# Sliding-window attention with sinks, then a gated layer: other queues and another order for the first loads of v, w_in, w_out, q and k

## The chip, the cores and the metric

The kernel runs on one core of a Trainium2 chip. Time is device time in microseconds (us) for one launch; lower is better. Five engines work side by side, each through its own instructions in order: PE (matmuls), ACT (exp, tanh, copies), DVE (elementwise and copies), POOL (casts, masks, and DMAs that change the type on their way) and SP (plain DMAs). All DMAs share 16 DMA engines, whichever engine asked for them. They wait for each other by semaphores that the program sets.

## What is computed

Attention over q, k and v of shape (4, 8, 768, 64) in f32, where a query sees the first 4 keys (the sinks) and the last 128 keys up to itself, and then a layer of 2048 gated units over the 3072 rows of 512 values:

```python
keep = (pos[None, :] < 4) | ((rel >= 0) & (rel < 128))
scores = where(keep, q @ k.T / 8, -1e9)
a = softmax(scores)                      # row maximum taken off, sum + 1e-9
x = (a @ v).transpose(0, 2, 1, 3).reshape(3072, 512)
h = x @ w_in                             # (512, 2048)
out = (h * sigmoid(beta * h)) @ w_out    # (2048, 512)
```

## The kernel before

**Units and blocks.** The 3072 rows are 8 tiles of 384 rows (`TT`). Attention goes by units: unit `n` is two heads of one tile, four units to a tile, 32 in all. Units 0 to 3 are the first tile (first half of batch 0), units 4 to 7 the second. The layer goes by blocks: block `i` is one tile by 128 of the 2048 gated columns, 16 blocks to a tile, each four products of 128 by 128 by 384 with `w_in16` (`hidden_matmul`, one per chunk `c` of the 512 columns of x). `tanh` (ACT) and `gate` (DVE) follow, then `project` multiplies with `w_out16`.

**A unit's way.** q and k land in f32 (`load_qk`, on SP's queue), `cast` makes them bf16 (`qk16`, three buffers), `transpose_in` turns them on PE and copies them from PSUM to `qkT`; `scores` multiplies them and takes exp on ACT into `E`; units 0 to 3 get their mask added on PE (`add_mask`), units 4 to 7 multiplied in on DVE. `attend` multiplies `E` with `v_aug` (v and a column of ones, in bf16), `normalise` divides, and `transpose_out` turns the result into `xT`, chunk `c` of which comes from the tile's unit `c`. So a tile's first block needs all four units, the last of them for its product `c = 3`. Units of the second half of a batch also have a product with the sinks' keys (`scores_sink`, `k_sink`) and values (`v_sink`); from unit 12 on q and k come through other paths that the change leaves alone.

**The first loads.** SP asks for q and k of units 0 to 3 at once. POOL's queue, whose DMAs cast f32 to bf16 on their way, brings v of units 0 to 3 straight into `v_aug` (`load_v`, three DMAs), w_in in four DMAs of four blocks' columns each (`load_w_in`), the sinks (`load_sinks`), v of units 4 to 7 and w_out in eight DMAs of two blocks each (`load_w_out`). q and k of units 4 to 7 are asked for on SP when the first w_in DMA has landed. POOL also casts k of units 0 to 3 and q and k of units 4 to 11, and fills `k_sink` and the masks of units 4 and up. ACT casts q of units 0 to 3.

**The order.** `Prog.op` records each operation with what it reads and writes, an engine, and a guessed duration (`busy`, and `lag` until the result can be used). `Prog.round` then plays the program: always the operation that can start first, by the guesses, is put next in its engine's order, and `Prog.landings` plays the DMA queues (a fixed time from issue to first data, `QUEUE`; bytes at a guessed rate; a share between queues that are busy together). The played order becomes the program, so a changed guess can change the order on every engine. In the new order as in the old each engine then works strictly through its list. Where PE has nothing to do before the first block, matmuls on ones (`P.filler`) fill the gap that the plan expects; they are part of the program and run whether or not the gap is there.

The place where units 0 to 3 hand over to the blocks, before the change:

```python
    for i in range(2):
        with P.together("pe"):
            for c in range(3):
                hidden_matmul(i, c)
        P.fill_until = P.fill_until or P.nodes[-1]
    transpose_out(3, acc[0], "acc0", "act")
    sink_keys()
```

Of the kernel before, what the change touches and what calls it, by code (L numbers as in the profile page):

```python
# [18 lines left out]
TT = 384  # L19
# [5 lines left out]
HEAD1 = 32  # L25

# [47 lines left out]
class Node:  # L74
# [3 lines left out]
                 "place", "dma", "mode", "work", "hard")  # L78

    def __init__(self, id, eng):  # L80
        self.id, self.eng = id, eng
        self.items = []
        self.busy = self.lag = 0.0
        self.preds = {}
        self.succs = []
        self.open = 0
        self.ready = self.done = 0.0
        self.place = None
        self.dma = None
        self.mode = 128  # L90
        self.work = 0.0
        self.hard = set()


class Prog:
# [12 lines left out]
    QUEUE = {"sp": (1200.0, 1.0), "act": (1200.0, 1.0), "gp": (2100.0, 3.0)}  # L108
    TAIL, MIX, RING = 900.0, 1.07, 8
# [27 lines left out]
    def op(self, eng, fn, r=(), w=(), x=(), dma=None, busy=100.0, lag=None, after=(), mode=None,  # L137
           seq=None):
# [28 lines left out]
        if dma is not None:  # L167
            self.dma_count[dma] = self.dma_count.get(dma, 0) + 16
            node.dma = (dma, self.dma_count[dma])
            node.work = lag  # L170
# [22 lines left out]
    def landings(self, placed):  # L193
# [9 lines left out]
        while True:  # L203
            now, later = [], []
            for q, ns in queue.items():
                if head[q] < len(ns):
                    at = ns[head[q]].place + self.QUEUE[q][0]
# [6 lines left out]
            whole = sum(self.QUEUE[q][1] for _, q in now)  # L214
            rate = {q: (self.MIX if len(now) > 1 else 1.0) * self.QUEUE[q][1] / whole for _, q in now}
# [12 lines left out]
    def round(self, took, freed):  # L228
# [10 lines left out]
        def best(e):  # L239
# [9 lines left out]
            n = min(c, key=lambda n: (max(n.ready, free[e]), n.id))  # L249
            at = max(n.ready, free[e])  # L250
            if n.dma is not None and issued[e] >= self.RING and freed:
                at = max(at, freed[e][issued[e] - self.RING] if issued[e] - self.RING < len(freed[e]) else at)
            return at, n
# [100 lines left out]
def bass_streamingllm_window__then__act_swish_beta_kernel(  # L354
# [42 lines left out]
    stage = {t: [sb(f"{t}_stage{z}", (128, 2, 6, D), F32) for z in range(4)] for t in "qk"}  # L397
    land = [sb(f"land{z}", (128, 2, 2, 3, 2, D), BF16) for z in range(4)]
    qk16 = [sb(f"qk16_{z}", (128, 2, 3, 2, D), BF16) for z in range(NQK)]
    v_aug = sb("v_aug", (128, 4, 2, 6, D + 2), BF16)  # L400
    v_sink = sb("v_sink", (128, NPAIR, 2, D1), BF16)
    k_rows = sb("k_rows", (NPAIR, NSINK, 2, D), BF16)
    k_sink = sb("k_sink", (128, NPAIR, 128), BF16)
    qkT = [sb(f"qkT{z}", (128, 2, 2, TT), BF16) for z in range(4)]
    E = [sb(f"E{z}", (128, 2, 768), BF16) for z in range(2)]
    E_sink = [sb(f"E_sink{z}", (128, TT), BF16) for z in range(2)]
# [25 lines left out]
    def transfer(size, rate, busy=470.0):  # L432
        return {"busy": busy, "lag": size / rate}
# [8 lines left out]
    def constants():  # L442
        fill("dve", ones32[:, :], 1.0, ["ones32"])
        op("act", lambda e: e.activation(scratch[:, :], ones32[:, 0:1], AF.Exp, bias=0.0, scale=1.0),
           r=["ones32"], w=["scratch"], busy=1500.0)
        fill("dve", ones[:, :], 1.0, ["ones"])
        fill("dve", zeros[:, :], 0.0, ["zeros"], busy=350.0)
        P.filler = (lambda e: e.matmul(acc[1][:, 0:128], ones[:, :], ones[:, :], start=True, stop=True),
# [66 lines left out]
    def load_qk(n, x, after=(), queue="sp"):  # L515
# [5 lines left out]
           dma=f"{name}{pb}_{half}", seq="loads " + queue, **transfer(2 * TT * D * 4, 335))  # L521

    def load_v(T, c, after=()):
# [6 lines left out]
           dma=f"vb{kb}", **transfer(H * 128 * D * 4, 256, 900.0))  # L530

    def land_qk(n, x, after=()):

        b, hp, half, pb = place(n)
        for hh in range(2):
# [3 lines left out]
               dma=f"l{pb}{half}{x}{hh}", **transfer(TT * D * 4, 256, 780.0))  # L539

    def land_v(n, after=()):
        b, hp, _, pb = place(n)
        half = place(n)[2]
        for hh in range(2):
# [3 lines left out]
               w=[("v", pb, 3 * half + c, hh) for c in range(3)], after=after, dma=f"lv{pb}{half}{hh}", **transfer(TT * D * 4, 256, 780.0))  # L548
# [13 lines left out]
    def load_w_in(c, cs, m, ms, after=()):  # L562
        here = slice(m * 128, (m + ms) * 128)
        op("gp", lambda e: e.dma_start(w_in16[:, c:c + cs, here], w_in_src[:, c:c + cs, here]), after=after,
           w=[("w_in", cc, mm) for cc in range(c, c + cs) for mm in range(m, m + ms)],
           dma=f"wi{c}_{m}", **transfer(cs * ms * 128 * 128 * 4, 345, 740.0))

    def load_w_out(m, ms, after=()):
        op("gp", lambda e: e.dma_start(w_out16[:, m:m + ms, :], w_out_src[:, m:m + ms, :]), after=after,
           w=[("w_out", mm) for mm in range(m, m + ms)],  # L570
           dma=f"wo{m}", **transfer(ms * 128 * NOUT * 4, 345, 740.0))

    def load_sinks(after=()):
        s = k[:, :, 0:NSINK, :].rearrange("b (g h) s d -> (b g) h (s d)", h=2)
        for hh in range(2):
            op("gp", lambda e, hh=hh: e.dma_start(k_rows[:, :, hh, :].rearrange("n s d -> n s d"),
# [414 lines left out]
```

## Time and profile before

| what | value |
|---|---|
| three runs | 229.54, 230.21 (median), 231.41 us |
| the profiled execution | 229.27 us, of which the profile's span is 227.5 |
| PE busy | 219.9 us (97% of the span), 1759 matmuls |
| ACT, DVE, POOL busy | 141.9, 132.2, 128.6 us |
| moved by DMA | 28.53 MB; queue q0 (POOL's) 62352 packets, q1 (SP's) 34304, q10 (ACT's) 176 |
| the chain that ended last | PE 87%, DMA 7%, ACT 2% |
| PE granted clock | 1.00 throughout |

The profile is one execution. Its times count from the start of the span; a line of the timeline gives start, length, engine, source line, operation and tiles, and in brackets how long the engine stood idle before it and for what. A busy PE is not PE at its peak, since matmuls overlap: what they cost in a row is the distance from one start to the next (0.16 us for a product of a block, 0.216 for one with w_out).

Where the first stage stands, in the answers of the trace: the eight loads of SP are issued at 0.81 to 4.73 us and land between 3.5 and 10.8; the three v loads are issued at 2.91, 4.98 and 6.96 and land at 10.2, 11.5 and 12.4; the four w_in loads are issued between 8.26 and 12.10 and land at 14.9, 17.7, 21.0 and 24.9; q and k of units 4 to 7 are issued from 14.90 on and land between 21.5 and 29.7; the w_out loads are issued from 26.41 on and land between 33.1 and 43.5. The exps of units 0 to 3 run on ACT from 8.41 to 17.8, the first product with w_out starts at 33.54, and the first block of the second tile at 47.11.

### The profile page before, as it was taken

The numbers are of one execution on the slowest core, as the hardware profiler recorded it, in microseconds if no ns is written. First come the engines' busy times: TensorE is split into PE (matmuls) and PEld (weight loads), VectorE is DVE, ScalarE is ACT, GpSimd is POOL, SyncE is SP. The second block draws the span as 40 slices with busy tenths as digits, with TensorE's granted clock in tenths as the row PEclk, the third lists the DMA queues.
The fourth block names the chain that finished last, engine by engine and source line by source line (L and its number), as shares of the span: only waits on it lengthen the run. The fifth ranks groups of instructions, "written<-read, shape, count | busy, mean of one in ns | idle before, by whom it ended". The sixth has DMA issues, their size and how long they took to land.

```text
span 227.5 us, 4449 instructions
## 1 busy us (share of the span) xinstructions
PE 219.9 (97%) x1759; PEld 121.7 (53%) x1759; DVE 132.2 (58%) x261; ACT 141.9 (62%) x223; POOL 128.6 (57%) x190
## 2 busy tenths in 40 slices
PE   7798989999999999999999999999999999999995
PEld 5355555545555555555555555555555555555544
DVE  5455887569977666566555555665656555443300
ACT  3655886477787666657767666656675764545411
POOL 7788996799975969494939679594600000000000
PEclk9999999999999999999999999999999999999999
DMA  6999999999997999999999989899932202111022
GB/s 163 204 193 220 246 192 208 244 208 176 122 98 117 104 131 151 119 125 128 140 102 142 115 122 162 118 101 147 140 41 63 64 19 63 49 46 46 9 86 92
DMA packets 96853, 28.53 MB, mean 125 GB/s; under 512 B 83376, under 2 KB 93888, under 8 KB 96832
## 3 DMA queue, kind: packets, MB, share of 16 engines
q0 software_dynamic: 62352, 11.32, 65.5%
q1 hardware_dynamic: 34304, 16.79, 33.8%
q8 instruction: 14, 0.23, 0.4%
q10 hardware_dynamic: 176, 0.14, 0.2%
q14 instruction: 7, 0.06, 0.1%
HBM read 27.34 MB, written 6.29 MB: 148 GB/s over the span
## 4 chain that ended last, share of the span: by engine, by line
PE 87%; DMA 7%; ACT 2%; POOL 1%; SPq 1%; issue 1%; DVE 0%; ACTq 0%
PE acc L809 34%; PE h_ps L780 33%; DMA v_aug<-in_v_dram 6%; PE s_ps L736 5%; PE s_ps L693 4%; PE acc L780 2%; PE h_ps L809 2%; DMA k_stage<-in_k_dram 2%; PE s_ps L725 1%; PE s_ps L637 1%; PE s_ps L665 1%; SPq L520 1%; PE s_ps L619 1%; POOL land L538 1%; PE h_ps L665 1%; POOL qk L606 1%
## 5 line engine op out<-in xcount | busy, mean ns | idle before, releaser
L788 ACT ACTIVATE th<-h_ps,beta_half 128x384 f32<-128x384 f32 x120 | 69.5, 581 | 55.6 <-PE h_ps L780 55.1
L809 PE MATMUL acc<-w_out,g 128*128 128x512 bf16 x368 | 101.5, 380 | 0.0
L780 PE MATMUL h_ps<-xT,w_in 128*128 128x384 bf16 x480 | 96.8, 326 | 0.0
L801 DVE SCALAR_TENSOR_TENSOR g<-th,h_ps 128x384 bf16<-128x384 f32 x120 | 65.6, 549 | 45.7 <-ACT th L788 45.0
L780 PEld LDWEIGHTS h_ps<-xT,w_in 128*128 128x128 bf16 x480 | 46.4, 98 | 40.4 <-DVE g L801 0.5
L809 PEld LDWEIGHTS acc<-w_out,g 128*128 128x128 bf16 x368 | 32.8, 98 | 28.0 <-issue 4.0
L538 POOL DMA_DIRECT2D land<-in_q_dram x40 | 30.9, 773 | 28.5 <-DVE rden L745 28.5
L547 POOL DMA_DIRECT2D v_aug<-in_v_dram x40 | 30.9, 773 | 0.0
L538 POOL DMA_DIRECT2D land<-in_k_dram x40 | 30.9, 773 | 0.0
L701 ACT ACTIVATE E<-s_ps 128x1536 bf16<-128x1536 f32 x20 | 28.8, 1442 | 0.3 <-PE s_ps L693 0.3
L707 DVE TENSOR_TENSOR E<-E,mask 128x1536 bf16<-128x1536 bf16 x20 | 19.2, 958 | 16.1 <-ACT E L701 16.1
L817 ACT ACTIVATE out_sb<-acc 128x512 f32<-128x512 f32 x23 | 13.7, 598 | 10.2 <-PE acc L809 10.0
L736 PE MATMUL s_ps<-v_aug,E 128*128 128x65 bf16 x384 | 19.4, 193 | 0.6 <-DMA v_aug<-in_v_dram 0.6
L736 PEld LDWEIGHTS s_ps<-v_aug,E 128*128 128x128 bf16 x384 | 17.0, 97 | 4.7 <-issue 1.4
L747 DVE TENSOR_TENSOR o_norm<-s_ps,rden 128x384 bf16<-128x384 f32 x32 | 17.7, 555 | 0.9
L673 ACT ACTIVATE E<-s_ps 128x768 bf16<-128x768 f32 x16 | 13.0, 809 | 2.3 <-PE s_ps L665 1.9
L626 DVE COPY qkT<-s_ps 128x768 bf16<-128x768 bf16 x10 | 9.5, 955 | 5.8 <-PE s_ps L619 5.7
L693 PE MATMUL s_ps<-qkT 64*128 64x256 bf16 (+2 forms) x144 | 10.1, 254 | 0.0
L745 DVE RECIPROCAL rden<-s_ps 128x6 f32<-128x6 f32 x32 | 6.1, 192 | 6.6 <-PE s_ps L736 6.3
L680 DVE TENSOR_TENSOR E<-E,mask 128x768 bf16<-128x768 bf16 x16 | 9.1, 581 | 1.5 <-ACT E L673 1.4
L528 POOL DMA_DIRECT2D v_aug<-in_v_dram x9 | 8.2, 915 | 2.3 <-DMA w_in<-in_moe_w_in_dram 1.7
L619 PE MATMUL s_ps<-ident,qk 128*128 128x128 bf16 x72 | 7.4, 227 | 2.1 <-POOL qk L606 0.7
(65 smaller groups left out, 145.4 us busy)
## 6 DMA issues: line engine op xcount, KB each, us to landing
out_dram<-out_sb SPq DMA_DIRECT2D x23, 256.0 KB, 2.6
q_stage<-in_q_dram SPq DMA_DIRECT2D x12, 192.0 KB, 7.1
k_stage<-in_k_dram SPq DMA_DIRECT2D x12, 192.0 KB, 8.0
w_in<-in_moe_w_in_dram POOLq DMA_DIRECT2D x4, 512.0 KB, 8.6
w_out<-in_moe_w_out_dram POOLq DMA_DIRECT2D x8, 256.0 KB, 8.4
land<-in_q_dram POOLq DMA_DIRECT2D x40, 48.0 KB, 3.5
land<-in_k_dram POOLq DMA_DIRECT2D x40, 48.0 KB, 3.8
v_aug<-in_v_dram POOLq DMA_DIRECT2D x40, 48.0 KB, 3.4
```

The source lines that it names most:

```text
L538: op("gp", lambda e, d=d, s=s: e.dma_start(d, s), w=[("land", pb, half, x, hh)], after=after, dma=f"l{pb}{half}{x}{hh}", **transfer(TT * D ...
L547: op("gp", lambda e, d=d, s=s: e.dma_start(d, s), w=[("v", pb, 3 * half + c, hh) for c in range(3)], after=after, dma=f"lv{pb}{half}{hh}", ...
L693: op("pe", lambda e, at=at, w=w, kb=kb, qb=qb, nq=nq, hh=hh, rows=rows, bank=bank: e.matmul(s_ps[:, 2 * hh + bank, at:at + w], keys_of(pb, ...
L701: op("act", lambda e: e.activation(E[z][:, :, :], src, AF.Exp, bias=0.0, scale=SCALE), x=list(S_NAMES), w=[("E", z, 0), ("E", z, 1)], **ac ...
L707: op("dve", lambda e: e.tensor_tensor(E[z][:, :, :], E[z][:, :, :], m.unsqueeze(1).to_broadcast([128, 2, 768]), ALU.mult), r=[("E", z, 0), ...
L736: last=(x == len(kbs) - 1): e.matmul(av_ps[:, at + hh * D1:at + hh * D1 + D1], E[z][:, hh, col:col + 128], v_aug[:, pb, hh, kb, 0:D1], sta ...
L747: op("dve", lambda e: e.tensor_tensor(o_norm[o][:, :, :, :].rearrange("p m h d -> p (m h) d"), src[:, :, 0:D], rden[z][:, :].unsqueeze(2). ...
L780: op("pe", lambda e: e.matmul(bank, w_in16[:, c, m * 128:(m + 1) * 128], xT[:, c, T * TT:(T + 1) * TT], start=(c == 0), stop=(c == 3)), r= ...
L788: op("act", lambda e: e.activation(th[i % 3][:, :], bank, AF.Tanh, bias=0.0, scale=beta_half[:, m:m + 1]), x=[name], r=["beta"], w=[("th", ...
L801: op("dve", lambda e: e.scalar_tensor_tensor(g[T % 2][:, m, :], th[i % 3][:, :], 1.0, bank, ALU.add, ALU.mult), r=[("th", i % 3)], x=[name ...
L809: op("pe", lambda e: e.matmul(bank[:, 0:width], g[T % 2][:, m, t * 128:(t + 1) * 128], w_out16[:, m, cols], start=(m == 0), stop=(m == NM ...
L817: op("act", lambda e: e.activation(out_sb[z][:, 0:width], bank[:, 0:width], AF.Copy, bias=0.0, scale=0.5), x=[name], w=[("out_sb", z)], ** ...
```

## The change

v of units 0 to 3 is no longer cast by its DMA. Six DMAs on ACT's queue (`load_v32`: four heads by 128 rows each) bring it in f32 to a new tile `v_stage`, and four casts on POOL (`cast_v`, one a unit) put it into `v_aug`. The exp table's first use on ACT moves behind these issues. w_in comes in two DMAs of eight blocks each, asked for when unit 0's and unit 2's v have been cast; the sinks' keys are asked for after unit 1's. q and k of units 4 to 7, the sinks' values, the first w_out DMA and v of units 4 to 7 wait for unit 3's cast v; POOL's fill of `k_sink` and its masks too. The other w_out DMAs wait for the two w_in DMAs.

For units 0 to 3, the cast of q goes from ACT to DVE, and `transpose_first` takes the place of `transpose_in`: q and k are turned into two banks, q copied out by ACT and k by DVE. Scores use up to three pairs of banks, `attend` and `normalise` the bank `acc1`. The four `transpose_out` come together after the attention of unit 3, and the first three products of three blocks (before: two) follow them. The product with beta's transpose moves to the front. The sinks' tiles get a height of their own, `SINKS`, which is 128, as it was.

In `Prog`, the guesses for DMA rates and shares change (a weight for each DMA in place of one for each queue), and an operation that waits for room in a DMA ring is now compared by that time too. So the order of operations also moves where the text of the kernel does not, up to the first blocks of the second tile and a little beyond.

```diff
+SINKS = 128
...
-    QUEUE = {"sp": (1200.0, 1.0), "act": (1200.0, 1.0), "gp": (2100.0, 3.0)}
-    TAIL, MIX, RING = 900.0, 1.07, 8
+    QUEUE = {"sp": 1200.0, "act": 1200.0, "gp": 2100.0}
+    TAIL, MIX, HEAVY, RING = 900.0, 1.1, 2.5, 8
...
-            whole = sum(self.QUEUE[q][1] for _, q in now)
-            rate = {q: (self.MIX if len(now) > 1 else 1.0) * self.QUEUE[q][1] / whole for _, q in now}
+            weight = {q: queue[q][head[q]].weight for _, q in now}
+            mix = self.MIX if len(now) > 1 and max(weight.values()) > self.HEAVY else 1.0
+            rate = {q: mix * w / sum(weight.values()) for q, w in weight.items()}
...
+    def load_v32(x, c):
+        src = v[0, 4 * x:4 * x + 4, c * 128:c * 128 + 128, :].rearrange("h p d -> p h d")
+        op("act", lambda e: e.dma_start(v_stage[:, c, 4 * x:4 * x + 4, :], src), w=[("v_stage", x, c)],
+           dma=f"v{x}{c}", seq="loads act", **transfer(4 * 128 * D * 4, 240, 520.0, 0.45))
+
+    def cast_v(n):
+        op("gp", lambda e: e.tensor_copy(v_aug[:, n, :, 0:3, 0:D].rearrange("p h c d -> p c h d"),
+                                         v_stage[:, :, 2 * n:2 * n + 2, :]),
+           r=[("v_stage", n // 2, c) for c in range(3)],
+           w=[("v", n, kb, hh) for kb in range(3) for hh in range(2)], busy=460.0, lag=100.0)
...
-            eng = "act" if n < 4 and x == 0 else "gp"
+            eng = "dve" if n < 4 and x == 0 else "gp"
...
+    def transpose_first(n):
+        z = n % NQK
+        for which, name in enumerate("qk"):
+            bank, at = ((tr_ps, "tr"), (av_ps, "av"))[which]
...
+            eng = "act" if which == 0 else "dve"
...
-    load_v(0, 0, [ADD[0][0]])
...
-            load_v(0, n + 1, [("k16", n)])
-    load_w_in(0, 4, 0, 4, [("q_stage", 2, 0)])
...
+    for c in range(6):
+        load_v32(c // 3, c % 3)
...
+    cast_v(0)
+    load_w_in(0, 8, [("v", 0, 0, 0)])
+    cast(2)
+    cast_v(1)
+    load_sinks(1, [("v", 1, 0, 0)])
...
+    cast(3)
+    cast_v(2)
+    load_w_in(8, 8, [("v", 2, 0, 0)])
+    cast_v(3)
...
-                    load_qk(y, x, [("w_in", 0, 0)])
+                    load_qk(y, x, [("v", 3, 0, 0)])
+            fill("gp", k_sink[:, :, :], 0.0, ["k_sink"], busy=1800.0, after=[("v", 3, 0, 0)])
+            masks([("v", 3, 0, 0)])
+            load_sinks(0, [("v", 3, 0, 0)])
+            load_w_out(0, 2, [("v", 3, 0, 0)])
             for c in range(3):
-                load_v(1, c, [("w_in", 0, 4)])
+                load_v(1, c, [("v", 3, 0, 0)])
...
+    for n in range(4):
+        transpose_out(n, *((av_ps, "av") if n % 2 else (tr_ps, "tr")), "dve" if n < 2 else "act")
+    for i in range(3):
...
-            for m in range(0, 8, 2):
-                load_w_out(m, 2, [("q_stage", 0, 1)])
+            for m in range(2, 8, 2):
+                load_w_out(m, 2, [("w_in", 0, 0)])
```

In the order that comes out, PE does blocks 0 to 7, the transposes of the sinks' keys, the 12 transposes of units 4 and 5 and one sink score before block 8, the first that reads the second half of w_in; before, the transposes of unit 4 stood behind 14 blocks' worth of products (56). On POOL the order from unit 3's cast v is: fill of `k_sink`, masks, two sink DMAs, one w_out DMA, three v DMAs, then the casts of q and k of units 4 and 5, two w_out DMAs, and the casts of unit 6.

More of the change, by code (lines that the diff above doesn't have):

```diff
@@ L90, in __init__ @@
         self.mode = 128
-        self.work = 0.0
+        self.work, self.weight, self.late = 0.0, 1.0, 0.0
         self.hard = set()
@@ L248, in best @@
                 return None
[L249 to L253, printed above, removed]
+            out = issued[e] - self.RING
+            room = freed[e][out] if freed and 0 <= out < len(freed[e]) else 0.0
+            at = {n.id: max(n.ready, free[e], room if n.dma is not None else 0.0) for n in c}
+            n = min(c, key=lambda n: (at[n.id], n.id))
+            return at[n.id], n
         while any(n.place is None for n in self.nodes):
@@ L644, in keys_read, with scores @@
     def keys_read(pb, half, runs):
-        return [("qkT", pb, x) for x in sorted({half, *(kb // 3 for kb, _, _ in runs)})]
-    def scores(n, c, banks, names):
+        return [("qT", pb), *(("qkT", pb, x) for x in sorted({half, *(kb // 3 for kb, _, _ in runs)}))]
+    def scores(n, c, names):
+        src = h_ps if names[0] == "h0" else s_ps[:, 0:2, :] if names[0] == "s0" else s_ps[:, 2:4, :]
+        banks = [src[:, hh, :] for hh in range(2)]
         _, _, half, pb = place(n)
```

152 lines of the change are left out of this document (79 added, 73 removed).

## The prediction

> **What bounds the kernel now.** First the page's 40 slices, 5.69 us each: PE, DMA share and GB/s.
>
> ```profile
> PE   7798989999999999999999999999999999999995
> DMA  6999999999997999999999989899932202111022
> GB/s 163 204 193 220 246 192 208 244 208 176 122 98 117 104 131 151 119 125 128 140 102 142 115 122 162 118 101 147 140 41 63 64 19 63 49 46 46 9 86 92
> ```
>
> PE is full from the fourth slice to the last. The DMA engines are full in the first ten, so the start is a matter of transfers, and after it the end is set by PE's work. Next the chain of waits (start, length, what), at the place where attention of units 0 to 3 hands over to the products with w_in:
>
> ```profile
> 18.66 0.59 PE acc L780 x3
> 19.25 0.49 PE h_ps L780 x3
> 19.74 0.18 PE acc L764 x3
> 19.95 0.49 ACT xT L768
> 20.48 0.34 PE acc L780
> ```
>
> Six products (0.98 us) run early and the rest flows from 20.48: as if the stream had begun at 20.48 - 0.98 = 19.5. Then PE's timeline, for the transposes of q and k of units 4 and 5:
>
> ```profile
> 28.95 0.50 PE L619 MATMUL s_ps<-ident,qk 128*128 128x128 bf16 x6
> ...
> 30.66 0.51 PE L619 MATMUL s_ps<-ident,qk 128*128 128x128 bf16 x6
> ```
>
> and POOL's timeline, which casts their operands:
>
> ```profile
> 12.83 1.83 POOL L440 MEMSET k_sink<- 128x2048 bf16 x1
> ...
> 17.95 2.68 POOL L528 DMA_DIRECT2D v_aug<-in_v_dram  x3 [1.72 <-DMA w_in<-in_moe_w_in_dram]
> ...
> 24.11 0.50 POOL L606 CAST qk<-q_stage 128x384 bf16<-128x384 f32 x1
> ...
> 25.96 0.51 POOL L606 CAST qk<-k_stage 128x384 bf16<-128x384 f32 x1 [0.28 <-DMA k_stage<-in_k_dram]
> ```
>
> Unit 5's k lands at 25.9, is cast by 26.5 and is used at 30.66: 4 us of slack, because PE has 14 blocks (of 4 products) from four w_in chunks ahead of it. Last, the DMA queues (packets, MB, share) from 16.0 to 18.4 us
>
> ```profile
> q0 software_dynamic: 473, 0.47, 121.2%
> ```
>
> and from 19 to 22 us:
>
> ```profile
> q0 software_dynamic: 391, 0.39, 77.6%
> q1 hardware_dynamic: 397, 0.29, 39.7%
> ```
>
> SP asks for q of unit 4 at 14.90, yet its queue q1 moves nothing before 18.5: 3.6 us behind a busy q0 (3.6 again at 35.64). Then the two alternate one to one: 16 engines x 3 us / 394 = 122 ns for a pair of a 2 KB w_in row and a 768 B q/k row. A w_in row alone takes 16 x 2.4 / 473 = 81 ns. From 24 to 28 us q1 and the small v rows of q0 move 1158 and 1186 packets: 55 ns a pair.
>
> **The change, part by part.**
>
> *Start.* SP's eight loads are 2048 packets; v adds 3072 packets of 256 B on ACT's queue. No row has two hardware queues with such packets; alone a 768 B packet takes 34 ns (first load) and a 256 B one 20 (around 60 us), 54 together, and the pair above 55. At one to one and 55 ns, q and k end at 2.8 + 128 x 0.055 = 9.9 (before: 10.8) and the first three v loads at 2.8 + 96 x 0.055 = 8.1, landed 8.4. POOL then goes in order: cast v 0.50, w_in issue 0.75, cast v 0.50, k2 0.52, two k_rows issues 1.05, k3 0.52, cast v 0.50, w_in issue 0.75, cast v 0.50: 14.0. ACT issues seven DMAs of some 0.5 before its table load (1.28, 0.20), free at 5.9 instead of 2.8; its first copy is ready about then. The q casts (ACT, 0.51 each) go to DVE, with no row: 0.35 (L768) to 0.56 (L747), I take 0.4, beside other work. The 0.96 us qkT copy becomes two halves, ACT 0.48 and DVE 0.5. Unit 3's k cast ends at 12.2, and the rest follows from rows: transposes and copy 0.9, scores 0.4, two exps 1.5, attend 0.5, normalise 0.8, transposes and copy 0.7, and waits for the banks of units 1 and 2: unit 3's last transposes at 17.2, then six filler matmuls (0.34). First product at 17.6 against 19.5: 1.9 earlier (1 to 3).
>
> *w_in in two.* The first half (512 rows of 4 KB) is issued at 8.9 and moves from about 11.1 (2.2 us after the issue, as the first v load: 2.91, 5.1). The row's 404 GB/s (473 x 2 KB in 2.4 us) gives 5.2 us: landed at 16.9, just in time. The second half follows on the same queue.
>
> *What comes next is late.* The first half feeds eight blocks: 8 x 0.65 + 0.2 (sink keys) = 5.4, so PE gets to unit 4's transposes at 23.0. In the new order these, unit 5's and a sink score stand ahead of block 8. They need q and k of units 4 and 5, asked for at 14.0 (before 14.9), so moving from 17.6 on, now against 4 KB rows. No row shows such a pair: between 122 ns (if size did not matter) and 122 + 81 = 203; I take 203, as the row's time grows with its bytes. The second half has 512 / 16 = 32 rows per engine, of which 8 are gone by 17.6 (from 16.3 on, 0.162 each); 24 x 0.203 ends at 22.5, landed 22.9. q/k have then moved 24 of the 64 packets per engine they need. Beside w_out's first load (16 pairs x 0.122) they get 16 by 24.5, and beside v rows the last 24 x 0.055 by 25.8: unit 5's k lands at 26.1 (25.0, with 122 ns pairs, to 27.2, if q1 starts later by the doubled time of the rows ahead of it). POOL casts it by 26.6, PE is through at 27.1.
>
> The Trainium skill ("DMA: Bandwidth & Descriptors", section "Anatomy of one DMA — SWDGE (gpsimd) path") fits a POOL-issued DMA as 2.0 us plus its bytes at 436 GB/s. Over 2.1 MB that is 6.8 us, the first half landed at 15.7; with rows of 0.150 in the steps above unit 5's k would land 1.0 earlier and the time be 229.9, an estimate by that page. The 404 GB/s of this trace stand in the sum.
>
> POOL is no quicker way: from 14.0, memset 1.8, masks 2.9, v_sink 1.3, w_out 0.73, three v issues 2.65 put its first q cast at 23.4, the fourth cast at 25.4.
>
> *Sum.* At 27.1 PE has done 8 blocks, 12 transposes and a sink score (0.34 + 0.34 + 0.16 = 0.84). Before, at 28.95, it had 14 blocks. Six blocks are 3.9: the new kernel reaches the same work at 27.1 + 3.9 - 0.84 = 30.2, 1.2 behind. From 28.95 to 46.77 (unit 8's transposes) PE before has 24 transposes 1.35, 8 products 1.3, four sink scores 0.65, eight scores of 0.27, 32 products of 0.216, four attends of 0.57, 12 transposes 0.7: 15.35 in 17.82, so 2.5 lost. Afterwards I count 0.7 lost at unit 6's transposes (its casts stand behind two w_out issues, 1.45), 0.3 at unit 7's, 1.0 in the units' chain: 2.0 (1.0 to 3.0), 0.5 back. Later w_out chunks come about 1.3 us earlier, which no wait of before asks for: 0. Net +1.2 - 0.5 = +0.7 us: the 1.9 gained at the start runs into the wait at 23.0. SINKS is 128, as the tiles were: that part changes nothing.
>
> The profiled execution took 229.27 (span 227.5 and 1.8 around it); the sum is 230.0 against it. The median shown is 230.21, 0.94 above: on that scale **230.9**. Its own range takes -1.1 and +1.1 from the landing and -1.0 and +1.0 from the later losses, not all at once: 229.4 to 232.5.
>
> **Rivals.**
>
> *The loads are in time.* If q1 starts 1.2 us after its issue, as the very first load did (issued 0.81, moving at 2.0), and 4 KB rows go as pairs of 2 KB ones, then 64 pairs x 0.122 from 15.2 end at 23.0; POOL's casts decide, 25.4, PE is through at 25.7: 1.4 less, 229.5; with only 1.0 lost later 228.5, with nothing lost 227.5. For it: the 4 us slack before. Against: 3.6 us, twice.
>
> *PE falls back to half clock.* At the start 128-column matmuls stand 107 ns apart until 5.8, then 56 (the PEclk row shows nothing of it). From 23.0 to 27.1 PE has 0.84 us of work in 4.1. If that is idle enough, the next 4 us go at half speed: +2, 232.9, slower than before. Against: 7.95 to 9.75 held only six transposes, and they kept 56 ns. It decides once the wait passes about 3 us.
>
> The Trainium skill ("TensorE: Matmul & The Clock Gate", "Part 1: The HAM clock gate") puts the fall to half rate after one idle window of about 3.4 us. No row here has such a gap; by that rule the 2 us are due only if the wait is one piece of that length, and unit 4's transposes, from 23.9 on, would split it.
>
> *4 KB rows move worse.* At 330 instead of 404 GB/s a row takes 0.198: the first half is gone at 17.5, the second, paired, 31 x 0.239 later at 25.0, and the remaining q/k packets (16 x 0.122 and 17 x 0.055) at 27.9, 2.1 later than above: 233.0. For it: no row of this size. Against: 768 B and 2 KB rows alone run at 361 and 404 GB/s.
>
> **Chances and range.** Forecast 0.47, loads in time 0.27, half clock 0.14, worse rows 0.12. One per cent is 2.3 us, about what can be told here (three runs spread 1.9). Faster by over 1% (under 227.9): 0.12 of the second case and 0.03 of the first: 0.15. Slower (over 232.5): 0.06 of the first, 0.12 of the third, 0.12 of the fourth: 0.30. Within: 0.55. The range takes in most of the second case and most of the last two: 227.8 to 233.7, with some 0.1 left out on each side.
>
> **What would show it.** The first w_in product at 17.6 and the first half landed by 17; SP's fifth load asked at 14.0, nothing of q1 moving before 17.6; two q0 packets of 4 KB against two of q1 from then; PE waiting for POOL's casts from 23.0, block 8 about 27; 56 ns spacing held. A first product later than 19.5, or block 8 before 25, makes the forecast wrong.

## The result and the profile after

The changed kernel takes 232.03 us (median; 230.88 to 236.49), the kernel before 229.63 on the same chips (228.54 to 231.41): a ratio of 1.0101, 95% interval 1.0078 to 1.0124, so 1% slower. Two of its fourteen executions, 234.46 and 236.49, count as slow and are left out of the ratio. The profiled execution took 232.1 us (span 230.4), 2.8 more than the profiled one of before. The page's slices, 5.76 us each:

```profile
PE   7899699979999999999999999999999999999995
DMA  6999999999997999999998989999972112111022
```

PE has a thin fifth slice (23 to 29 us) where before it was full. The chain of waits shows what ends last in it (start, length, what; gaps left out):

```profile
20.75 0.49 PE acc L814 x3
21.23 0.97 PE h_ps L814 x6
...
22.41 1.17 ACT th L822 x3
...
26.50 0.59 ACT th L822
...
27.12 0.55 DVE g L835
27.67 0.88 DVE qkT L641
...
28.59 0.52 PE s_ps L634 x6
```

The first w_in products come at 20.6. The chain then leaves PE: it goes through ACT's tanh of blocks 0 to 7 and the last of DVE's gates for them, then DVE's copy of unit 4's transposes, and only then back to PE, which transposes unit 5. PE's timeline (start, length, what, and in brackets the idle time before it and what ended it):

```profile
20.58 0.65 PE L814 MATMUL acc<-xT,w_in 128*128 128x384 bf16 x3
...
26.24 0.50 PE L634 MATMUL s_ps<-ident,qk 128*128 128x128 bf16 x6
28.59 0.51 PE L634 MATMUL s_ps<-ident,qk 128*128 128x128 bf16 x6 [1.85 <-DVE qkT L641]
28.94 0.33 PE L670 MATMUL s_ps<-qkT,k_sink 128*128 128x384 bf16 x1
29.10 0.81 PE L814 MATMUL acc<-xT,w_in 128*128 128x384 bf16 x4
```

Units 4 and 5 are transposed into the same bank of PSUM (tr), the memory that PE writes its results to. Unit 5's transposes must wait until DVE has copied unit 4's out of it; DVE runs in order and has the gates first; and block 8, whose weights landed at 24.94, stands behind unit 5 on PE. Before, two blocks lay between the two units (28.95 and 30.66) and hid the same copy, as PE's and DVE's timelines of the kernel before show:

```profile
29.29 0.81 PE L780 MATMUL h_ps<-xT,w_in 128*128 128x384 bf16 x4
29.94 0.81 PE L780 MATMUL acc<-xT,w_in 128*128 128x384 bf16 x4
29.65 0.95 DVE L626 COPY qkT<-s_ps 128x768 bf16<-128x768 bf16 x1
```

POOL's timeline of the changed kernel shows how near the casts were:

```profile
27.21 0.51 POOL L621 CAST qk<-k_stage 128x384 bf16<-128x384 f32 x1 [0.53 <-DMA k_stage<-in_k_dram]
```

Unit 5's k is cast by 27.7, 0.9 before PE can use it. The same kernel profiled a second time (232.31 us, span 230.6) took another way to the same end:

```profile
18.48 0.65 PE L814 MATMUL acc<-xT,w_in 128*128 128x384 bf16 x3
...
24.57 0.34 PE L634 MATMUL s_ps<-ident,qk 128*128 128x128 bf16 x3 [0.27 <-POOL qk L621]
25.42 0.34 PE L634 MATMUL s_ps<-ident,qk 128*128 128x128 bf16 x3 [0.51 <-POOL qk L621]
26.81 0.94 PE L634 MATMUL s_ps<-ident,qk 128*128 128x128 bf16 x6 [1.05 <-DVE qkT L641]
27.55 0.53 PE L670 MATMUL s_ps<-qkT,k_sink 128*128 128x384 bf16 x1
27.87 1.49 PE L814 MATMUL acc<-xT,w_in 128*128 128x384 bf16 x4
```

Here the start is 2.1 earlier, PE waits for casts and for the copy, and then four products take 1.49 instead of 0.81: half rate. The windows view has a granted clock of 0.50 from 26.82 to 30.23 and 1.00 on both sides. The page's clock row (tenths of full rate per slice) shows it in the fifth and sixth slice:

```profile
PEclk9999889999999999999999999999999999999999
```

PE also begins at half rate in every profile used here: 128-column matmuls stand 107 ns apart and later 56. The change came at 13.0 us in profile 1 and between 6.1 and 7.4 in profile 2; the page's clock row does not show this one.

To compare all runs, I worked out from PE's records when the same amount of matmul work was reached (columns streamed, fillers left out; 27 to 28 records that are missing in each trace but before's are counted by the program's order), as time behind the kernel before (profile 1 is the execution of 232.10 us, profile 2 that of 232.31):

```
reached before at us    24.6   26.7   28.9   44.2   46.8    end
changed, profile 1     +1.5   +3.5   +3.3   +2.2   +3.3   +2.9
changed, profile 2     -0.6   +3.4   +3.2   +2.2   +3.5   +3.1
qk_early               +0.7   +2.7   +2.4   +1.4   +2.8   +2.4
fill_wait              -0.4   +1.7   +2.0   +1.1   +1.7   +1.8
filler_more            -0.7   +3.9   +5.0   +4.0   +5.3   +4.9
w_in_four              -0.6   -0.2   -0.5   -1.2   -0.9   -0.7
order_only             +0.8   +0.9   +0.6    0.0   -0.6   -0.7
order_qk2              -0.8   +0.2    0.0   -0.8   -1.3   -1.4
```

One stretch makes most of the loss, from 24.6 to 26.7 on that scale: +2.0 in one profile, where a late start had made 1.5 before it, and +4.0 in the other. What follows gives back some of it and takes some again.

### The profile page after: what moved, and what is told of

It is laid out like the page before. It is cut to its first block, busy times and chain, and to the rows that moved or that the text cites. A ratio compares the mean times of both kernels' runs of the same rounds, so it can differ in the third digit from the quotient of the medians.

```text
span 230.4 us, 4457 instructions
## 1 busy us (share of the span) xinstructions
PE 219.8 (95%) x1748; PEld 123.7 (54%) x1775; DVE 132.2 (57%) x264; ACT 141.3 (61%) x224; POOL 125.5 (54%) x189
## 4 chain that ended last, share of the span: by engine, by line
PE 86%; ACT 5%; DVE 3%; issue 3%; DMA 2%; POOL 0%; SPq 0%; ACTq 0%; POOLq 0%
PE acc L843 33%; PE h_ps L814 32%; PE s_ps L770 5%; PE s_ps L727 4%; ACT th L822 3%; PE s_ps L700 2%; DMA k_stage<-in_k_dram 2%; PE h_ps L843 2%; PE s_ps L759 1%; PE acc L450 1%; PE s_ps L670 1%; PE s_ps L798 1%; DVE g L835 1%; PE s_ps L634 1%; DVE E L714 1%
## 5 line engine op out<-in xcount | busy, mean ns | idle before, releaser
L843 PE MATMUL acc<-w_out,g 128*128 128x512 bf16 x341 | 94.8, 380 | 1.7 <-issue 0.6
L561 POOL DMA_DIRECT2D v_aug<-in_v_dram x40 | 30.9, 774 | 0.0
L735 ACT ACTIVATE E<-s_ps 128x1536 bf16<-128x1536 f32 x20 | 28.9, 1443 | 0.0
L770 PE MATMUL s_ps<-v_aug,E 128*128 128x65 bf16 x336 | 16.8, 193 | 0.8 <-DVE E L714 0.7
L770 PEld LDWEIGHTS s_ps<-v_aug,E 128*128 128x128 bf16 x336 | 15.1, 97 | 4.2 <-issue 1.3
L781 DVE TENSOR_TENSOR o_norm<-s_ps,rden 128x384 bf16<-128x384 f32 x28 | 15.5, 555 | 0.8
L714 DVE TENSOR_TENSOR E<-E,mask 128x768 bf16<-128x768 bf16 x16 | 9.8, 615 | 1.0 <-ACT E L707 0.7
L621 POOL CAST qk<-k_stage 128x384 bf16<-128x384 f32 x12 | 6.1, 511 | 5.9 <-DMA k_stage<-in_k_dram 5.9
L759 PE MATMUL s_ps<-v_sink,E_sink 128*128 128x130 bf16 x48 | 9.3, 219 | 0.0
L779 DVE RECIPROCAL rden<-s_ps 128x6 f32<-128x6 f32 x28 | 5.4, 192 | 6.0 <-PE s_ps L770 6.0
L727 PEld LDWEIGHTS s_ps<-qkT 64*128 64x128 bf16 x144 | 4.9, 94 | 7.1 <-issue 6.4
```

What stands on the lines that cost most here:

```text
L561: op("gp", lambda e, d=d, s=s: e.dma_start(d, s), w=[("v", pb, 3 * half + c, hh) for c in range(3)], after=after, dma=f"lv{pb}{half}{hh}", ...
L727: op("pe", lambda e, at=at, w=w, kb=kb, qb=qb, nq=nq, hh=hh, rows=rows, bank=bank: e.matmul(s_ps[:, 2 * hh + bank, at:at + w], keys_of(pb, ...
L735: op("act", lambda e: e.activation(E[z][:, :, :], src, AF.Exp, bias=0.0, scale=SCALE), x=list(S_NAMES), w=[("E", z, 0), ("E", z, 1)], **ac ...
L770: last=(x == len(kbs) - 1): e.matmul(av_ps[:, at + hh * D1:at + hh * D1 + D1], E[z][:, hh, col:col + 128], v_aug[:, pb, hh, kb, 0:D1], sta ...
L781: op("dve", lambda e: e.tensor_tensor(o_norm[o][:, :, :, :].rearrange("p m h d -> p (m h) d"), src[:, :, 0:D], rden[z][:, :].unsqueeze(2). ...
L843: op("pe", lambda e: e.matmul(bank[:, 0:width], g[T % 2][:, m, t * 128:(t + 1) * 128], w_out16[:, m, cols], start=(m == 0), stop=(m == NM ...
```

## Experiments

Line numbers in the experiments' profiles are shifted by a few where lines were added. Every ratio is to the kernel before on the same chip. The expectations name theories: by 'start' v's new way slows the first loads, and late operands of unit 5 hold block 8; by 'DVE order', which came after qk_early, DVE's late copy holds it.

**filler_more**: more fillers before 14 us, at the same places.

```
-                    for _ in range(int((start - at - 60.0) * 0.8 / cost)):
+                    count = int((start - at - 60.0) * 0.8 / cost)
+                    for x in range(count):
                         f = Node(-1, "pe")
-                        f.items.append((fn, None, [self.filler[2]]))
+                        more = (count + 1) // 2 if x == count - 1 and at < 14000.0 else 0
+                        f.items.extend([(fn, None, [self.filler[2]])] * (1 + more))
```

> The changed kernel with each run of filler matmuls before 14 us half as long again (written out at the same places, the order of everything else as it is), so that PE has fewer gaps. Rival 'half clock': PE goes to 56 ns a 128-column matmul at 6 to 9 us instead of 13, the first product moves from 20.6 to 19.6 or earlier, and the time falls by 1 us or more, to 231 or less. Theory 'start': PE may be at full rate sooner, the first product may gain 0.3 to 0.8, but unit 4's and 5's casts stay at 24.7 to 27.2 and block 8 at 29.0 to 29.2; the time stays within 0.4 of the changed kernel's 232.0.

Measured: 232.51 us (1.0119, 1.0078 to 1.0160). The first product came at 18.38 (20.58 in profile 1), and the time did not fall, not even in the three executions whose granted clock stayed at 1.00 (231.81, 232.34 and 232.49): the start's half rate is not what the change costs. PE's timeline, of an execution of 234.12 us and so the slowest of its set, shows where the gain went:

```profile
26.05 0.34 PE L636 MATMUL s_ps<-ident,qk 128*128 128x128 bf16 x3 [1.54 <-POOL qk L623]
27.45 0.83 PE L636 MATMUL s_ps<-ident,qk 128*128 128x128 bf16 x6 [1.05 <-DVE qkT L643]
28.07 0.53 PE L672 MATMUL s_ps<-qkT,k_sink 128*128 128x384 bf16 x1
28.39 1.49 PE L816 MATMUL acc<-xT,w_in 128*128 128x384 bf16 x4
```

The wait for casts and copy grew by what the start gained, and half rate followed it, longer than in the changed kernel.

**qk_early**: SP's loads of q and k of units 4 to 7 wait for unit 0's cast v; the order on every engine is unchanged.

```
-                    load_qk(y, x, [("v", 3, 0, 0)])
+                    load_qk(y, x, [("v", 0, 0, 0)])
```

The wait was exchanged after planning, so that the planner could not answer it.

> The changed kernel with one wait changed: SP's loads of q and k of units 4 to 7 wait for unit 0's cast v instead of unit 3's; the order on every engine is the same. They are asked for at about 9.6 us instead of 15.4. Theory 'start': the loads then move beside both w_in halves, some 0.2 us a pair of rows; unit 5's k lands by 20 instead of 27.2, the first w_in half 0.8 to 2 later (19.7 to 21 for 18.9), and block 8, freed of the wait, at 27.0 to 27.8 instead of 29.1; time 1.2 to 2.0 less than the changed kernel's: 230.0 to 230.8. Rival 'order': block 8 is earlier but the time is not, since later waits take it: within 0.5 of 232. Rival 'w_in': the first half now comes so late (after 22) that the first product is held by it and the time is as long or longer.

Measured: 231.68 us (1.0079, 1.0041 to 1.0117). Unit 5's k landed at 19.91, 7 us earlier, yet PE's timeline is the old one:

```profile
19.75 0.66 PE L818 MATMUL acc<-xT,w_in 128*128 128x384 bf16 x3 [1.29 <-DMA w_in<-in_moe_w_in_dram]
...
25.41 0.50 PE L638 MATMUL s_ps<-ident,qk 128*128 128x128 bf16 x6
27.77 0.51 PE L638 MATMUL s_ps<-ident,qk 128*128 128x128 bf16 x6 [1.85 <-DVE qkT L645]
28.11 0.33 PE L674 MATMUL s_ps<-qkT,k_sink 128*128 128x384 bf16 x1
28.27 0.81 PE L818 MATMUL acc<-xT,w_in 128*128 128x384 bf16 x4
```

The wait at unit 5 is the same 1.85 us, though POOL, which now waited for no load, had cast the last operand by 25.8 (23.89 to 25.8 for the four casts, as the prediction reckoned for POOL alone: 23.4 to 25.4). Block 8 is 8.52 behind the first product here and in profile 1 of the changed kernel (29.10 - 20.58). This ended my theory that late loads hold block 8. (The second w_in half landed at 26.73 here, still ahead of the 27.77 at which unit 5's transposes began.) DVE's timeline shows the copy straight behind the last gate:

```profile
24.99 1.20 DVE L839 SCALAR_TENSOR_TENSOR g<-th,h_ps 128x384 bf16<-128x384 f32 x2
26.29 0.55 DVE L839 SCALAR_TENSOR_TENSOR g<-th,acc 128x384 bf16<-128x384 f32 x1
26.76 0.95 DVE L645 COPY qkT<-s_ps 128x768 bf16<-128x768 bf16 x1
```

**w_in_four**: four w_in DMAs of four blocks, two at each place.

```
-    load_w_in(0, 8, [("v", 0, 0, 0)])
+    for m in (0, 4):
+        load_w_in(m, 4, [("v", 0, 0, 0)])
```

> The changed kernel with w_in in four DMAs of four blocks instead of two of eight, two issued at each of the two places; the planner then puts units 4's and 5's transposes behind blocks 9 and 11 instead of in front of block 8. Theory 'start': the first product stays near 20 (unit 3's chain, not w_in, holds it), but PE has blocks 8 to 11 to do while unit 4's and 5's q and k come, so most of the wait of 26 to 29 us goes: 1.0 to 1.8 less, 230.2 to 231.0. Rival 'w_in size': if 4 KB rows were what makes the loads late, 2 KB rows should land the first blocks' weights earlier and the first product moves to 19 or earlier. Rival 'no effect': the wait only moves behind block 11, within 0.5 of 232.

Measured: 229.31 us (0.9979, 0.9953 to 1.0006), 2.7 less than the changed kernel and more than expected. Two things differ: the DMAs, and the order that the planner makes of them. The next run parts them.

**order_only**: all DMAs as in the changed kernel; the planner alone is told a higher rate for the second w_in half. Its own schedule had that half landing at 27.1 (the traces: 24.4 and 24.9), and unit 5's k at 23.1 (the traces: 26.6 and 27.2), and so put units 4 and 5 ahead of block 8; with 23.9 it puts unit 4 behind block 8 and unit 5 behind block 11.

```
+        rate = 400 if m == 0 else 800
...
-           dma=f"wi{m}", late=0.0 if m else 800.0, **transfer(DM * ms * 128 * 4, 400, 740.0, 3.0))
+           dma=f"wi{m}", late=0.0 if m else 800.0, **transfer(DM * ms * 128 * 4, rate, 740.0, 3.0))
```

> The changed kernel with every DMA as it is (w_in in two of 4 KB rows, the same waits); only the planner is told that the second w_in half comes sooner, so that it puts unit 4's transposes behind block 8 and unit 5's behind block 11 instead of both in front of block 8. Theory 'DVE order': the wait at unit 5's transposes goes (under 0.5 us), block 8 follows block 7 at once, 5.4 to 6 behind the first product, and the time falls by 1.7 to 2.7: 229.3 to 230.3, as the kernel with four w_in DMAs did (229.31). Rival 'w_in size': it is the four DMAs that made that kernel fast; here block 8 waits for the second half (landed 24.9) and the time stays above 231.2. Rival 'half clock': no stretch at half rate was in that profile, so no part of it.

Measured: 228.27 us (0.9961, 0.9940 to 0.9983), 3.8 less than the changed kernel's first set, 4.3 less than its second (232.56, beside this one on the same chip), 1 us more than was expected, and faster than the kernel before. PE's timeline:

```profile
19.93 0.65 PE L815 MATMUL acc<-xT,w_in 128*128 128x384 bf16 x3
...
24.94 1.46 PE L815 MATMUL acc<-xT,w_in 128*128 128x384 bf16 x8
26.24 0.50 PE L635 MATMUL s_ps<-ident,qk 128*128 128x128 bf16 x6
26.58 1.46 PE L815 MATMUL h_ps<-xT,w_in 128*128 128x384 bf16 x8
27.88 0.81 PE L815 MATMUL acc<-xT,w_in 128*128 128x384 bf16 x4
28.53 0.50 PE L635 MATMUL s_ps<-ident,qk 128*128 128x128 bf16 x6
```

No row has an idle time: block 8 begins at 25.59, 5.7 behind the first product, and three blocks lie between units 4 and 5 while DVE copies (26.94 to 27.9). The loads are those of the changed kernel (unit 5's k landed at 26.27, the second half at 24.04). So order alone takes the loss away, and two DMAs of 4 KB rows are no worse than four. By the table the profiled executions of the two orders lie 3.6 apart: 0.7 is there by 24.6 (the starts), 2.0 comes in the stretch to 28.9, and 0.9 behind it, where the order differs too. No run gave unit 5 a bank of its own, which would try the bank without the order.

**v_by_pool**: v of units 0 to 3 by POOL's three casting DMAs as before, w_in still in two.

```
-    for c in range(6):
-        load_v32(c // 3, c % 3)
+    load_v(0, 0, [ADD[0][0]])
...
-    cast_v(0)
-    load_w_in(0, 8, [("v", 0, 0, 0)])
+    load_w_in(0, 8, [("q_stage", 2, 0)])
...
-    cast_v(2)
-    load_w_in(8, 8, [("v", 2, 0, 0)])
-    cast_v(3)
+    load_w_in(8, 8, [("k16", 0)])
```

The other two load_v stand between the casts as before; SP's loads for units 4 to 7 wait for the first w_in half, POOL's fill, masks and later loads for unit 0's cast k.

> Undoes the v part: v of units 0 to 3 comes by POOL's three casting DMAs as before the change, with no v on ACT's queue and no cast v on POOL; the two w_in DMAs wait for unit 2's q and unit 0's k cast, q and k of units 4 to 7 for the first w_in half; the rest is the changed kernel. Theory 'start': v's 256 B rows on a second hardware queue slow the first loads, these delay POOL's casts, issues and SP's asks, and unit 5's late q and k then hold block 8. By it q and k of units 0 to 3 land by 10.9 us again (12.5 in the changed kernel), the first product with w_in is at 19.0 to 19.8 (20.6), and the time is 1.5 to 2.5 us less than the changed kernel's, 229.5 to 230.5. Rival 'half clock': PE's half speed until 13 us is the cost; it goes away here only if PE is busier at the start. Rival 'order': the planner's new order on PE and the new constants cost the time whatever the loads do: within 0.5 of 232.

Measured: 230.30 us (1.0038, 1.0009 to 1.0067), in the range that theory 'start' gave, with its first product at 18.20, earlier than that. But the planner also put unit 4's q transposes ahead of block 5, so this says little of v's route. Its profiled execution (232.41, well above the median) has PE waiting and then at half rate:

```profile
24.91 0.34 PE L634 MATMUL s_ps<-ident,qk 128*128 128x128 bf16 x3 [2.15 <-POOL qk L621]
25.09 2.29 PE L814 MATMUL h_ps<-xT,w_in 128*128 128x384 bf16 x8
```

**w4_v_by_pool**: v by POOL with w_in in four; it differs from w_in_four in v's route and in the waits that hang on it.

```
-    for c in range(6):
-        load_v32(c // 3, c % 3)
+    load_v(0, 0, [ADD[0][0]])
...
-    load_w_in(0, 8, [("v", 0, 0, 0)])
+    for m in (0, 4):
+        load_w_in(m, 4, [("q_stage", 2, 0)])
```

> Four w_in DMAs with v of units 0 to 3 by POOL's three casting DMAs as before the change, q and k of units 4 to 7 asked for at the first w_in chunk. Beside the kernel that differs from it in v's route alone (229.31), in an order without the wait. Theory 'v's route costs': q and k of units 0 to 3 land earlier (10.6 for 11.5), the first product is 0.5 to 1 earlier and the time 228.3 to 229.0. Rival 'v's route pays': the first w_in chunk waits behind v on the one queue of POOL (landed 15.8 or later for 14.4) and the time is 229.6 to 230.5. Null: within 0.3 of 229.3.

Measured: 229.66 us (1.0007, 0.9984 to 1.0030) against 0.9979 for w_in_four. The profiled execution took 973.99 us, so its times are not used; its order can be read, and it moved here too: unit 4's q transposes stand behind 6 blocks, in w_in_four behind 10. The intervals overlap: no cost of v's route can be told, but no run parts the route cleanly from the order.

**before_v**: the kernel before with v's route alone changed.

```
-    load_v(0, 0, [ADD[0][0]])
+    for c in range(6):
+        load_v32(c // 3, c % 3)
...
             cast(3)
+            cast_v(2)
+            cast_v(3)
```

The casts of v of units 0 and 1 follow cast(1) and cast(2).

> The kernel before with one part of the change alone: v of units 0 to 3 uncast by six DMAs on ACT's queue and cast by POOL; w_in in its four DMAs with their old waits, q casts on ACT as before. Theory 'v's route is not the cost': first product within 1 us of 19.5, time within 1.0 of the kernel before (229.4), since the order behind it has 14 blocks ahead of unit 4's transposes to take up the difference. Rival 'start': the first loads are slowed, the first product comes 1 us or more later and the time is 230.4 or more.

Measured: 231.11 us (1.0073, 1.0049 to 1.0096), outside 1.0 of before. Yet the first product came at 19.02, 0.4 later than before's (18.59), so not by the rival's way. PE waits elsewhere:

```profile
27.71 0.24 PE L602 MATMUL s_ps<-ident,k_rows 16*128 16x16 bf16 x4 [1.05 <-DMA k_rows<-in_k_dram]
```

In my version POOL asks for k_rows at 16.36, behind the memset; that wait is most of the 1.4 by which it falls back at 26.7. So it says nothing clean of v's route.

**after_again**: the changed kernel, for the second profile above.

> The changed kernel once more, for a second profile. In the first profile unit 1's k landed at 8.63 and PE ran at half rate to 13.0; three other kernels with the same first section had it at 7.3 to 7.8 and PE at full rate by 6 to 8.3. If that first start was one draw among several, the first product is at 18.4 to 19.8 here (20.6 there). Theory 'start': block 8 then moves with it. Theory 'DVE order' (formed from the kernel whose q and k came early and which was hardly faster: unit 5's transposes wait 1.85 us for DVE's copy of unit 4's, which stands behind the gates of blocks 0 to 7, and block 8 is 8.52 us behind the first product in both): block 8 is 8.5 behind the first product, unless unit 4's k cast (26.1 at the latest seen) holds it longer; time near 232 either way.

Measured: 232.56 us (1.0126, 1.0084 to 1.0169). Block 8 came 9.4 behind the first product, held longer by the casts as the second theory allowed. The half rate behind it had been expected by neither.

**fill_wait**: 27 fillers written into the wait, order and DMAs unchanged.

```
+            if n.id in self.waits:
+                f = Node(-2 - n.id, "pe")
+                f.items = [self.idle] * self.waits[n.id]
+                placed.append(f)
```

> The changed kernel with its order and all its DMAs, and 27 filler matmuls written into the wait: 3 ahead of unit 4's q transposes, 8 ahead of its k transposes, 16 ahead of unit 5's. In the second profile of the changed kernel the wait (24.0 to 26.8) was followed by 3.5 us of matmuls at half rate (320 ns for 384 columns), in the first, with a later start, by none. Theory 'both': the wait itself costs some 2 us and stays, the half rate behind it goes; block 8 at 27.7 to 28.2, full rate after it, time 0.6 to 1.4 less than the changed kernel's 232.0 to 232.6: 230.8 to 231.6. Rival 'wait alone': the half rate cost nothing (PE catches up), within 0.4 of 232.3. Rival 'clock alone': all of the loss was the half rate, 229.5 or less.

Measured: 231.84 us (1.0094, 1.0057 to 1.0131). In its profile (231.07, its fastest execution) PE stays at full rate and block 8 comes at 27.30:

```profile
25.28 1.06 PE L457 MATMUL s_ps<-ones 128*128 128x128 bf16 x16
26.68 0.62 PE L642 MATMUL s_ps<-ident,qk 128*128 128x128 bf16 x6 [0.35 <-DVE qkT L651]
27.14 0.33 PE L680 MATMUL s_ps<-qkT,k_sink 128*128 128x384 bf16 x1
27.30 0.81 PE L824 MATMUL acc<-xT,w_in 128*128 128x384 bf16 x4
```

Profile against profile it is 1.0 to 1.2 us faster than the changed kernel, as 'both' says; the median is only 0.2 (first set) to 0.7 (second) lower, and the intervals overlap. 'Clock alone' is out: most of the loss stays with PE at full rate. How much half rate costs can be read from the mean granted clock that every execution has on record: in the profiles 3.41 us at half rate make it 0.993 (profile 2), and 6.83 us 0.985 (filler_more). All six executions of fill_wait are at 1.00. Of the changed kernel's eighteen, ten are at 1.00 (median 231.46), six at 0.993 (median 232.6) and two at 0.985. So half rate costs some 1.1 us where it strikes for 3.41 us, and against executions without it the fillers bring nothing. The kernel before has executions at 0.993 too, and 229.1 to 229.3 is the median of those at 1.00 in each of its three later sets: some 2.2 of the loss is there without half rate. Where an execution without a profile went to half rate is not shown.

**order_more** and **order_qk2**: order_only with the fillers of filler_more, and order_only with the loads of q and k at unit 2's cast v.

```
-                    load_qk(y, x, [("v", 3, 0, 0)])
+                    load_qk(y, x, [("v", 2, 0, 0)])
```

That is order_qk2's line, exchanged after planning; order_more's are those of filler_more.

> The changed kernel with unit 4's and 5's transposes behind blocks 8 and 11 (228.27) and, besides, each run of early fillers half as long again. If PE's half rate at the start (to 13.5 in the last profile of that order, first product 19.9) decides the first product, it comes at 18.4 to 18.6 and the time falls by 0.5 to 1.5, to 226.8 to 227.8. Rival: the earlier start runs into the casts of units 4 and 5 (24.5 to 26.8) or into the second w_in half (24.1), no change within 0.4.

> The same order (unit 4 behind block 8, unit 5 behind block 11), with SP's loads of q and k of units 4 to 7 asked for at unit 2's cast v instead of unit 3's, about 1.5 us earlier. In that order unit 5's casts are done at 26.8 and used at 28.5, so earlier loads should bring nothing: within 0.4 of 228.3, the second w_in half some 0.3 to 0.8 later. Rival 'loads': if the asks at unit 3's cast v are a cost of the change by themselves, 0.5 to 1.5 less.

Measured: 228.68 us (0.9964, 0.9938 to 0.9989) and 229.01 (0.9982, 0.9958 to 1.0006), beside order_only's 0.9961. The earlier start of order_more (18.09) ran into a wait of 0.99 for unit 4's k cast, as its rival said. order_qk2, with its first product at 18.30, waited 0.84 at block 8 for the second w_in half, which order_only, begun at 19.93, did not. Earlier asks brought nothing that can be told; the profiled execution of order_qk2 was its best (227.83), so its row in the table above flatters it.

**w4_more**: the lines of w_in_four and those of filler_more together.

> Four w_in DMAs and each run of early fillers half as long again. With the wait at units 4 and 5 gone, an earlier start should count: if fillers bring the first product from 18.1 (four DMAs) to 17.6 or so, the time is 0.3 to 0.6 less than 229.3. Rival: the start is held by the loads and unit 3's chain, no change within 0.3 of 229.3; or fillers delay the work behind them: up to 0.5 more.

Measured: 228.44 us (0.9967, 0.9943 to 0.9990) against 0.9979: no difference that can be told, and the first product at 18.19 was no earlier than without (18.07).

## Why the prediction was right and wrong

The time lay in the range. By its ratio it stands at the edge of "slower by over 1%", which had 0.30; as a time, 232.03 is under the 232.5 that the case was given, and so in "within", which had 0.55. The forecast's own value was 1.1 us low. As a difference it was further off: +0.7 was forecast, +2.4 measured. The time hides part of that by luck: the sum stood on a median of before of 230.21 from three runs, which came out at 229.63 in fourteen. The structure held: the end is set by a wait ahead of block 8 in which PE has nothing else in its order. The sum did not: +1.2 was forecast where the new kernel meets the work of 28.95, and +3.3 and +3.2 were measured in the two profiles.

*Start: 1.9 earlier, first product at 17.6.* Mis-sized: 20.58 and 18.48, and 18.1 to 19.9 in the other kernels with v uncast and the same w_in halves whose first product did not wait for w_in. Against before's 19.5, as the forecast reckoned it, that is 1.1 later in profile 1 and 1.0 earlier in profile 2. One cause is the pair of v and q/k, taken one to one at 55 ns. The DMA view from 3 to 9 us in profile 1 shows (packets, MB, share):

```profile
q1 hardware_dynamic: 1478, 1.07, 63.0%
q10 hardware_dynamic: 2549, 0.63, 49.1%
```

1.7 packets of 256 B went for each one of 768 B, so q and k ended at 12.5 (12.0 in profile 2) instead of 9.9, and POOL's casts and SP's asks moved with them (asks at 15.37 and 14.66 for 14.0). The other goes with PE's half rate at the start, which I had not seen as variable: order_only, with loads as early as profile 2's (unit 1's k at 7.82 and 7.61) but half rate until 12.7, began 1.45 later.

*w_in in two.* The first half landed at 18.89 and 18.21 instead of 16.9, the second at 24.94 and 24.41 instead of 22.9: issued 0.4 to 1.1 later, its first packet 1.65 after the issue (2.2 was taken), its 32 rows an engine 185 ns apart because the first ones went beside the tail of the first loads, and landed 1.35 after the last packet began (0.6 was taken). From 13 to 18 us, with little beside it, a row took 164 ns (16 x 5 / 488), as the 162 of the forecast. The Trainium skill ("DMA: Bandwidth & Descriptors", "Anatomy of one DMA — SWDGE (gpsimd) path") would give 6.8 us from issue to landing, an estimate by its fit; the trace has 8.9 in both profiles, beside other loads, and does not agree. It cost nothing here: PE shows no wait for either half.

*Asks and pairs.* Right. q1 moved its first packet 3.85 us after the ask in profile 1 and 3.95 in profile 2 (3.6 forecast), and from 20 to 23 us the DMA view has the two queues one to one, 197 ns a pair (16 x 3 / 243) where 203 was taken:

```profile
q0 software_dynamic: 242, 0.50, 86.9%
q1 hardware_dynamic: 244, 0.18, 24.1%
```

Unit 5's k landed at 27.16 and 26.64, inside the 25.0 to 27.2 given.

*"POOL casts it by 26.6, PE is through at 27.1."* This step failed. It priced the operands of the two transposes and not the bank that they share. Freeing it takes DVE's copy, and DVE's order has the gates of blocks 0 to 7 first, which ACT's tanh (0.48 each) fed until 27.1. qk_early shows this wait alone, at full size with the operands long there; in profile 1 PE is through at 29.10 for the 27.1 forecast, two later; in profile 2 casts and copy both hold, and PE is through at 27.87. By luck the two limits lie within 1 us of each other, so that block 8 came near the 27 that was named in profile 2.

*Half rate in the wait.* Priced at 2 us with a chance of 0.14, time 232.9: it is what profile 2 shows, at 232.31, and profile 1 does not. It decided earlier than the "about 3 us" I gave: see below. I had counted it and the forecast as alternatives; half rate comes on top of the wait in some executions (eight of the changed kernel's eighteen have a granted clock under 0.999), and 3.41 us of it cost some 1.1 where 2 were given (under fill_wait).

*Later losses, 0.5 back.* Measured: 0.4 back in profile 1 (3.3 to 2.9), 0.1 in profile 2. About right.

*What the forecast did not ask:* whether the order was needed. It took units 4 and 5 ahead of block 8 as given by the new loads. order_only shows that the new loads bear an order with blocks between the two units, as the old one had; the whole change is then worth 1.0 us against the kernel before (228.27 to 229.29).

## What to carry to other kernels

When an in-order engine meets two tasks that use one buffer back to back, price the task that empties the buffer, with everything queued ahead of it on its own engine, as well as the operands. Where a schedule is made from estimated landings, compare the estimates with the trace: one landing put 2 to 3 us too late turned a gain of 0.4% into a loss of 1%. And an earlier start is worth only what the next wait leaves of it.

## What the runs showed of the hardware

The rate of PE at the start varied between executions whose programs are alike there: 128-column matmuls, first 107 ns apart, were first seen 56 apart at 7.4 (changed kernel, profile 2), 7.0 (qk_early), 8.3 (w_in_four), 13.0 (profile 1) and about 12.7 us (order_only). The Trainium skill ("TensorE: Matmul & The Clock Gate", "Part 1: The HAM clock gate") says that the activity window runs freely and that the number of slow matmuls varies by run. These traces agree, with a wider spread than its half a microsecond.

Back to half rate PE went in three of the profiles: profile 2 (0.50 from 26.82 to 30.23), filler_more (26.56 to 33.39) and v_by_pool (25.57 to 28.98), so for 3.41, 6.83 and 3.41 us. In profile 2 it fell 2.5 us into a wait that had two bursts of three transposes in it (24.3 to 26.8), in filler_more 2.4 us into one with the same (24.2 to 26.6), and in v_by_pool 0.7 us behind a wait of 2.15 us in one piece. PE kept full rate after 1.85 us in one piece (profile 1 and qk_early). The wait need not be one piece: six transposes in the midst of it did not prevent the fall. Counted by the distance from one start to the next, PE had some 1.1 to 1.2 us of matmuls in the 3.41 us before each fall, and in profile 1 and qk_early no less than 1.4 in any 3.41 us around the wait. By the section of the Trainium skill named above the fall comes after an idle window of about 3.4 us; in these three traces it came with a third of such a stretch at work.
